# Another order of work, and another PSUM layout, for the first sequence of an attention and feed-forward kernel

## The chip, the cores and the metric

The kernel runs on one core of a Trainium2 chip. The metric is the device time of one execution in microseconds (us), the median of several runs. A profile of one execution gives every instruction's engine, start and length; its times count from the first instruction. PE is the matmul engine (TensorE), PEld its loading of weights, DVE is VectorE, ACT ScalarE, POOL GpSimd, SP the engine that issues most transfers.

## The reference

All data is float32. Attention with a threshold over 8 sequences of 576 tokens with 8 heads of 64, and then two matrices with an ELU between them. The weights come as 64-bit floats and are converted on the chip.

```python
# q, k, v: (8, 8, 576, 64);  tau = 0.02;  w_in: (512, 2048);  w_out: (2048, 512)
scores = (q @ k.transpose(0, 1, 3, 2)) / sqrt(64)
thresh = scores.max(-1, keepdims=True) - tau
scores = where(scores >= thresh, scores, -1e9)
attn = exp(scores - scores.max(-1, keepdims=True))
attn = attn / (attn.sum(-1, keepdims=True) + 1e-9)
x = (attn @ v).transpose(0, 2, 1, 3).reshape(4608, 512)
h = x @ w_in
out = where(h > 0, h, exp(minimum(h, 0)) - 1) @ w_out
```

## The kernel before

The kernel has three stages. In the first, the first sequence's attention is computed alone, since there is nothing yet to put through the two matrices; some weights are converted meanwhile. In the second, attention goes on beside the first sequence's matrices and the rest of the conversions. In the third and longest, attention and matrices share the engines until only matrices are left. The change touches the first stage.

A sequence has four pairs of heads, and a pair five steps: i = 0 to 3 are 128 queries of two heads each, and i = 4 holds the last 64 queries of both heads as one block of 128 rows, handled as one head. So a sequence has 20 steps. For each step and head the first stage does the following (S = 576, HALF = 288, P = 128; cuts are marked):

```python
psum = {"t": tile_pool(name="ps_t", bufs=2, space=PSUM)}      # transposes and values: 2 banks
psum["s"] = tile_pool(name="ps_s0", bufs=3, space=PSUM)       # scores: 3 tiles of 2 banks
# ...
def scores(pr, i, hs):
    # ...
    if "f" in psum and not apart:                              # second stage: one tile for both heads
        both = psum["s"].tile([P, 2, 2, 512], FP32, name="sc")
        scs = {h: both[:, h] for h in hs}
    else:                                                      # first and third stage: one tile a head
        scs = {h: psum["s"].tile([P, 2, 512], FP32, name="sc") for h in hs}
    for a in range(2):
        for h in hs:
            # ... r: the 64 partitions of head h
            nc.tensor.matmul(scs[h][:, a, :HALF], qs[r], kT[r, k0 : k0 + HALF], start=True, stop=True)

def exponentials(pr, i, hs):
    nc.vector.tensor_reduce(st["mx"][:, cs], src[:, :, :, :HALF], axis=AX.XY, op=ALU.max)
    nc.gpsimd.tensor_scalar(st["nb"][:, cs], st["mx"][:, cs], nkeep, 1.0, ALU.mult, ALU.mult)
    nc.gpsimd.tensor_scalar(st["th"][:, cs], st["mx"][:, cs], 1.0, ntau, ALU.mult, ALU.add)
    for h in hs:
        e = att.tile([P, 2, HALF], FP32, name="e")
        nc.scalar.activation(e, st[h][:, :, :HALF], AF.Exp, bias=st["nb"][:, h : h + 1], scale=keep)

def masks(pr, i, hs):
    for h in hs:                                               # keeps e where the score is over the threshold; sums
        nc.vector.scalar_tensor_tensor(wv, sc[:, :, :HALF], st["th"][:, h : h + 1], e, ALU.is_ge, ALU.mult,
                                       accum_out=sm[:, h : h + 1])
    nc.vector.tensor_scalar(sm[:, cs], sm[:, cs], 1e-9, None, ALU.add)
    nc.vector.reciprocal(rs[:, cs], sm[:, cs])

def normalize(pr, i, hs):
    for h in hs:
        nc.gpsimd.tensor_scalar(wv, wv, st["rs"][:, h : h + 1], 1.0, ALU.mult, ALU.mult)
```

The weighted scores w are then transposed on TensorE in three portions of four, four and one block (turn_parts), each into a tile of psum["t"] that ScalarE copies out. After steps 1 and 4 of a pair the values are multiplied in (17 matmuls into a tile of psum["t"]); part 0 covers steps 0 and 1, part 1 the steps 2 to 4.

```python
def values(pr, part):
    pv = psum["t"].tile([P, 512], FP32, name="pv", tag="rt")
    nc.tensor.matmul(pv[:, :n], vd, wT[:, :, NC], start=True, stop=False, skip_group_check=True)
    for c in range(NC):
        for h in range(2):
            nc.tensor.matmul(pv[h * D : (h + 1) * D, g0 * T : g1 * T], vm[:, h, c], ..., start=False, ...)
    return lambda: values_out(pr, part, pv)                    # copies pv out on ScalarE
```

The loop of the first stage goes head by head, and the compiler's scheduler may move instructions in it:

```python
load(0); prep(0); load(1)
begin(*heads[0])                                 # begin: scores and exponentials; finish: masks and normalize
for n, (pr, i, hs) in enumerate(heads):          # 36 heads: one entry for each head of each step
    if n + 1 < len(heads):
        begin(*heads[n + 1])
    # ... loads of weights
    if n >= 12 and n % 4 == 0:
        convert_w()                              # six pieces of 128 x 512 weights in this stage
    finish(pr, i, hs)
    if len(turned) > 1:
        behind(*turned.popleft())                # values
    if n and hs == [0]:
        turn(*heads[n - 1][:2])                  # transposes of the step before
        turned.append(heads[n - 1][:2])
    if hs == [1]:
        ahead(pr, i + 1)                         # loads, and q and k of the next pair
```

Of the kernel before, what the change touches and what calls it, by code (L numbers as in the profile page):

```python
# [10 lines left out]
FP32 = mybir.dt.float32  # L11
# [8 lines left out]
def kernel(  # L20
# [47 lines left out]
    first = ExitStack()  # L68
    psum["s"] = first.enter_context(tc.tile_pool(name="ps_s0", bufs=3, space=PSUM))

# [7 lines left out]
    tau_sb = const.tile([P, 1], FP32, name="tau_sb")  # L78
    nc.sync.dma_start(tau_sb, tau.to_broadcast([P, 1]))
    pos = const.tile([P, 1], FP32, name="pos")  # L80
    nc.vector.tensor_scalar(pos, tau_sb, 0.0, None, ALU.is_ge)
    keep = const.tile([P, 1], FP32, name="keep")
    nc.vector.tensor_scalar(keep, pos, SCALE, None, ALU.mult)
    nkeep = const.tile([P, 1], FP32, name="nkeep")
    nc.vector.tensor_scalar(nkeep, pos, -SCALE, None, ALU.mult)
    far = const.tile([P, 1], FP32, name="far")
    nc.vector.tensor_scalar(far, pos, -FAR, FAR, ALU.mult, ALU.add)
    ntau = const.tile([P, 1], FP32, name="ntau")
    nc.vector.tensor_tensor(ntau, tau_sb, far, ALU.max)
    nc.vector.tensor_scalar(ntau, ntau, -1.0 / SCALE, None, ALU.mult)  # L90

# [64 lines left out]

    def convert_w():
        i = progress[1]
        if i >= progress[0]:
            return  # L160
        for f in (convert_top, convert_rest, convert_add, convert_abs, convert_end):
            f(i)
        load_w()


    raws, pairs = {}, {}


    def load(pr, parts=("qm", "km", "v"), shared=False):
        b, j = divmod(pr, NPAIR)  # L170
        tiles = raws.setdefault(pr, {})
        for name, src in (("qm", q), ("km", k)):
            if name not in parts:
                continue
            m = tiles[name] = raw.tile([P, S // T, T], FP32, name="qm" if shared else name)
            for i in range(2):
                for d in range(2):
                    r = (2 * i + d) * T
                    nc.sync.dma_start(
                        m[r : r + T],  # L180
                        src[b, 2 * j + i].rearrange("(j t) d -> t j d", t=T)[:, :, d * T : (d + 1) * T],
                    )
        if "v" not in parts:
            return
        vm = tiles["vm"] = raw.tile([P, 2, NC, D], FP32, name="vm", bufs=2)
        vd = tiles["vd"] = vds[pr % NVD]
        for i in range(2):
            vh = v[b, 2 * j + i]
            nc.sync.dma_start(vm[:, i], vh[:MAIN].rearrange("(c p) d -> p c d", p=P))
            r = slice(i * TAIL, (i + 1) * TAIL)  # L190
            nc.sync.dma_start(vd[r, r], vh[MAIN:])
# [25 lines left out]

    wTs, xts, open_steps, turns = {}, {}, {}, {}
    apart = []


    def scores(pr, i, hs):
        qT, kT, qd = pairs[pr]
        if hs[0] == 0:
            open_steps[pr, i] = {
                **{x: small.tile([P, 2], FP32, name=x) for x in ("mx", "nb", "th", "sm", "rs")},
            }
        st = open_steps[pr, i]
        if "f" in psum and not apart:
            both = psum["s"].tile([P, 2, 2, 512], FP32, name="sc")  # L230
            scs = {h: both[:, h] for h in hs}
        else:
            scs = {h: psum["s"].tile([P, 2, 512], FP32, name="sc") for h in hs}
        for a in range(2):
            for h in hs:
                k0 = a * HALF + (0 if h else TAIL)
                r, qs = (slice(h * D, (h + 1) * D), qT[:, i * P : (i + 1) * P]) if i < NC else (slice(0, P), qd)
                nc.tensor.matmul(scs[h][:, a, :HALF], qs[r], kT[r, k0 : k0 + HALF], start=True, stop=True)  # L238
        if len(hs) == 2 and not apart:
            st["both"] = both  # L240
        for h in hs:
            st[h] = scs[h]

    def exponentials(pr, i, hs):
        st = open_steps[pr, i]
        cs = slice(hs[0], hs[-1] + 1)
        src = st["both"] if len(hs) == 2 else st[hs[0]].unsqueeze(1)
        nc.vector.tensor_reduce(st["mx"][:, cs], src[:, :, :, :HALF], axis=AX.XY, op=ALU.max)
        nc.gpsimd.tensor_scalar(st["nb"][:, cs], st["mx"][:, cs], nkeep, 1.0, ALU.mult, ALU.mult)  # L249
        nc.gpsimd.tensor_scalar(st["th"][:, cs], st["mx"][:, cs], 1.0, ntau, ALU.mult, ALU.add)  # L250
        for h in hs:
            e = att.tile([P, 2, HALF], FP32, name="e")
            nc.scalar.activation(e, st[h][:, :, :HALF], AF.Exp, bias=st["nb"][:, h : h + 1], scale=keep)  # L253
            st[h] = st[h], e

    def masks(pr, i, hs):
# [5 lines left out]
        for h in hs:  # L262
            sc, e = st.pop(h)
            wv = w[:, h * S : (h + 1) * S].rearrange("p (a n) -> p a n", a=2)
            nc.vector.scalar_tensor_tensor(wv, sc[:, :, :HALF], st["th"][:, h : h + 1], e, ALU.is_ge, ALU.mult,  # L265
                                           accum_out=sm[:, h : h + 1])
# [3 lines left out]
    def normalize(pr, i, hs):  # L270
        st = open_steps[pr, i]
        for h in hs:
            wv = st["w"][:, h * S : (h + 1) * S]
            nc.gpsimd.tensor_scalar(wv, wv, st["rs"][:, h : h + 1], 1.0, ALU.mult, ALU.mult)  # L274

    def transpose(dst, src):
# [11 lines left out]
    def turn_parts(pr, i):  # L288
        w = open_steps.pop((pr, i))["w"]
        wT, g0 = turned_tile(pr, i)  # L290
# [4 lines left out]
        def room():  # L295
            return psum["t"].tile([P, NC, P], FP32, name="rt", tag="rt")

# [240 lines left out]

    def begin(*step):
        scores(*step)  # L540
        exponentials(*step)

    def finish(*step):
        masks(*step)
        normalize(*step)

    def ahead(pr, i):
        if i == 2 and pr + 1 < NP:
            prep(pr + 1)
        if i == 3 and pr + 2 < NP:  # L550
            load(pr + 2, ("qm", "km"))
        if i == 3 and pr + 1 < NP and pr:
            load(pr + 1, ("v",))

    load(0)
    prep(0)
    load(1)

    heads = [(pr, i, [h]) for pr, i in steps[:per_seq] for h in heads_of(i)]
    turned = deque()  # L560
    begin(*heads[0])
    for n, (pr, i, hs) in enumerate(heads):
        if n + 1 < len(heads):
            begin(*heads[n + 1])
        if n == 2:
            load_w()
            load_w()
        if n >= 12 and n % 4 == 0:
            convert_w()
        finish(pr, i, hs)  # L570
        if len(turned) > 1:
            behind(*turned.popleft())
        if n and hs == [0]:
            turn(*heads[n - 1][:2])
            turned.append(heads[n - 1][:2])
        if hs == [1]:
            ahead(pr, i + 1)
    first.close()
    for name, bufs in (("s", 1), ("f", 2)):
        psum[name] = banks.enter_context(tc.tile_pool(name=f"ps_{name}", bufs=bufs, space=PSUM))  # L580

    while len(turned) > 1:
        behind(*turned.popleft())

# [161 lines left out]
    with tc.manual_schedule():  # L746
# [335 lines left out]

        def max_of(pr, i, h):
            st = open_steps[pr, i]
            nc.vector.tensor_reduce(st["mx"][:, h : h + 1], st[h][:, :, :HALF], axis=AX.XY, op=ALU.max)  # L1085

        def bound_of(pr, i, h):
            st = open_steps[pr, i]
            nc.gpsimd.tensor_scalar(st["th"][:, h : h + 1], st["mx"][:, h : h + 1], 1.0, ntau, ALU.mult, ALU.add)  # L1089

        def exp_of(pr, i, h):
            st = open_steps[pr, i]
            nc.scalar.mul(st["nb"][:, h : h + 1], st["mx"][:, h : h + 1], nkeep)  # L1093
            e = att.tile([P, 2, HALF], FP32, name="e")
            nc.scalar.activation(e, st[h][:, :, :HALF], AF.Exp, bias=st["nb"][:, h : h + 1], scale=keep)  # L1095
            st[h] = st[h], e

        def mask_of(pr, i, h):
            st = open_steps[pr, i]
            if h == 0:  # L1100
                st["w"] = wpool[0].tile([P, 2 * S], FP32, name="w")
            sc, e = st.pop(h)
            wv = st["w"][:, h * S : (h + 1) * S].rearrange("p (a n) -> p a n", a=2)
            nc.vector.scalar_tensor_tensor(wv, sc[:, :, :HALF], st["th"][:, h : h + 1], e, ALU.is_ge, ALU.mult,  # L1104
                                           accum_out=st["sm"][:, h : h + 1])

        def reciprocal_of(pr, i, hs):
            st = open_steps[pr, i]
            cs = slice(hs[0], hs[-1] + 1)
            nc.vector.tensor_scalar(st["sm"][:, cs], st["sm"][:, cs], 1e-9, None, ALU.add)  # L1110
            nc.vector.reciprocal(st["rs"][:, cs], st["sm"][:, cs])  # L1111

        begun = [0.0]
# [100 lines left out]
        spaces = [raw.tile([P, S // T, T], FP32, name="qm")]  # L1214
        spaces += [att.tile([P, 2, HALF], FP32, name="e") for _ in range(2)]
        spaces = [x.rearrange("p a n -> p (a n)") for x in spaces]
        spaces += [raw.tile([P, 2, NC, D], FP32, name="vm", bufs=2).rearrange("p h c d -> p (h c d)") for _ in range(2)]
        w = wpool[0].tile([P, 2 * S], FP32, name="w")
# [54 lines left out]
```

## Time and profile before

| | |
|---|---|
| time, median of 3 runs | 1387.97 us (1381.94 to 1388.02) |
| profiled execution, span | 1379.2 us |
| busy: PE, DVE, POOL, ACT | 1333.0, 1060.4, 834.1, 624.7 us |
| mean granted clock of TensorE | 0.996 |
| first score matmul | 8.44 us |
| last mask of the first sequence | from 102.09 us, 0.82 us long |
| first max of the second sequence | 106.33 us |

Busy times are sums over the whole span; PE's is modelled, and its matmuls overlap. The first stage is some 8% of the span. A record of a float32 score or value matmul counts twice (x4 is two matmuls); a transpose counts once. In a group or a piece of the timeline, "L265" is the line of the kernel, then come engine, operation, the tiles written and read, and shapes; in brackets stands how long the engine was idle before, and what ended that.

### The profile page before, as it was taken

The numbers are of one execution on the slowest core, as the hardware profiler recorded it, in microseconds if no ns is written. First come the engines' busy times: TensorE is split into PE (matmuls) and PEld (weight loads), VectorE is DVE, ScalarE is ACT, GpSimd is POOL, SyncE is SP. The second block draws the span as 40 slices with busy tenths as digits, with TensorE's granted clock in tenths as the row PEclk, the third lists the DMA queues.
The fourth block names the chain that finished last, engine by engine and source line by source line (L and its number), as shares of the span: only waits on it lengthen the run. The fifth ranks groups of instructions, "written<-read, shape, count | busy, mean of one in ns | idle before, by whom it ended". The sixth has DMA issues, their size and how long they took to land.

```text
span 1379.2 us, 21964 instructions
## 1 busy us (share of the span) xinstructions
PE 1333.0 (97%) x6566; PEld 989.4 (72%) x6566; DVE 1060.4 (77%) x2364; ACT 624.7 (45%) x1371; POOL 834.1 (60%) x1345
## 2 busy tenths in 40 slices
PE   7897989999999999999999999999999999999998
PEld 4554745747777777777777777777777777888886
DVE  6787885988878887888788878888888875545433
ACT  4675655225454544445453635364535452312320
POOL 4667774878657564757475747665575656525423
PEclk9999999999999999999999999999999999999999
DMA  5245452688788989798889888897889885321211
GB/s 114 58 92 148 133 148 44 189 244 253 228 257 229 261 226 257 209 257 247 236 229 256 245 224 245 221 263 215 232 229 270 215 255 166 122 69 62 95 58 31
DMA packets 316342, 259.82 MB, mean 188 GB/s; under 512 B 208320, under 2 KB 272320, under 8 KB 316224
## 3 DMA queue, kind: packets, MB, share of 16 engines
q1 hardware_dynamic: 316224, 258.42, 67.4%
q8 instruction: 53, 0.87, 0.3%
q14 instruction: 65, 0.53, 0.1%
HBM read 167.84 MB, written 90.51 MB: 187 GB/s over the span
## 4 chain that ended last, share of the span: by engine, by line
PE 74%; DVE 9%; ACT 5%; POOL 4%; DMA 3%; issue 3%; SPq 1%; DVEq 0%; POOLq 0%; ACTq 0%
PE f L1001 27%; PE f L846 20%; PE sc L238 11%; PE pv L388 8%; PE pv L384 2%; PE f L435 2%; PE f L475 2%; ACT e L1095 2%; DVE w L265 2%; DMA there<-x 2%; ACT e L253 1%; DVE mx L1085 1%; PE rt L277 1%; POOL wtop L143 1%; POOL w L274 1%
## 5 line engine op out<-in xcount | busy, mean ns | idle before, releaser
L274 POOL TENSOR_SCALAR w<-w,rs 128x576 f32<-128x576 f32 x288 | 246.1, 860 | 108.1 <-DVE rs L1111 75.2
L1085 DVE TENSOR_REDUCE mx<-sc 128x1 f32<-128x576 f32 x207 | 148.0, 751 | 83.4 <-PE sc L238 83.4
L238 PE MATMUL sc<-kT,qT 64*128 64x288 f32 x1024 | 182.3, 441 | 20.8 <-DVE w L265 11.5
L348 DVE STREAM_TRANSPOSE x<-w 128x512 f32<-128x512 f32 (+1 forms) x350 | 182.5, 567 | 8.2 <-POOL w L274 8.2
L1093 ACT ACTIVATE nb<-mx,nkeep 128x1 f32<-128x1 f32 x207 | 61.4, 297 | 253.2 <-DVE mx L1085 253.2
L1095 ACT ACTIVATE e<-sc,nb,keep 128x576 f32<-128x576 f32 x207 | 172.0, 831 | 6.9
L1104 DVE SCALAR_TENSOR_TENSOR w<-sc,th,e 128x576 f32<-128x576 f32 x207 | 163.1, 810 | 8.7 <-ACT e L1095 0.4
L238 PEld LDWEIGHTS sc<-kT,qT 64*128 64x128 f32 x1024 | 100.8, 191 | 85.4 <-issue 52.4
L846 PE MATMUL f<-xt,sw 128*128 128x256 f32 x512 | 128.9, 389 | 0.5 <-DVE g L868 0.5
L846 PE MATMUL f<-xt,w_in_sb 128*128 128x256 f32 x512 | 124.5, 382 | 0.3 <-ACT w L860 0.2
L1089 POOL TENSOR_SCALAR th<-mx,ntau 128x1 f32<-128x1 f32 x207 | 54.4, 264 | 112.1 <-DVE mx L1085 111.8
L846 PE MATMUL f<-x,w_in_sb 128*128 128x256 f32 x448 | 109.0, 382 | 5.5 <-ACT g L912 5.5
L846 PEld LDWEIGHTS f<-xt,sw 128*128 128x128 f32 x512 | 93.3, 190 | 28.9 <-issue 13.5
L253 ACT ACTIVATE e<-sc,nb,keep 128x576 f32<-128x576 f32 x81 | 65.1, 830 | 103.5 <-POOL nb L249 102.6
L846 PEld LDWEIGHTS f<-xt,w_in_sb 128*128 128x128 f32 x512 | 96.1, 190 | 18.9 <-ACT xs L400 4.6
L1001 PE MATMUL f<-w_out_sb,s 128*128 128x256 f32 x448 | 109.4, 387 | 0.0
L1001 PE MATMUL f<-w_out_sb,g 128*128 128x256 f32 x448 | 107.2, 382 | 0.0
L1001 PE MATMUL f<-t,s 128*128 128x256 f32 x448 | 106.6, 380 | 0.3 <-POOL s L938 0.3
L846 PEld LDWEIGHTS f<-x,w_in_sb 128*128 128x128 f32 x448 | 84.1, 190 | 21.2 <-ACT g L912 10.2
L1001 PEld LDWEIGHTS f<-w_out_sb,s 128*128 128x128 f32 x448 | 82.3, 190 | 23.0 <-issue 13.2
L1001 PEld LDWEIGHTS f<-w_out_sb,g 128*128 128x128 f32 x448 | 84.0, 190 | 15.9 <-ACT ge L879 3.1
L865 POOL TENSOR_TENSOR u<-u,w 128x256 f32<-128x256 f32 x64 | 48.9, 765 | 76.4 <-ACT u L860 76.4
(162 smaller groups left out, 2572.2 us busy)
## 6 DMA issues: line engine op xcount, KB each, us to landing
there<-x SPq DMA_DIRECT2D x500, 144.0 KB, 4.3
wTb<-there SPq DMA_DIRECT2D x75, 576.0 KB, 4.7
wTa<-there SPq DMA_DIRECT2D x50, 576.0 KB, 4.4
sw<-win_sums SPq DMA_DIRECT2D x62, 384.0 KB, 4.6
t<-wout_sums SPq DMA_DIRECT2D x45, 512.0 KB, 5.5
qm<-in_q_dram SPq DMA_DIRECT2D x128, 72.0 KB, 4.2
vm<-in_v_dram SPq DMA_DIRECT2D x64, 128.0 KB, 4.3
wst<-in_moe_w_in_dram SPq DMA_DIRECT2D x16, 512.0 KB, 4.5
```

The costliest lines, as they stand in the source:

```text
L238: nc.tensor.matmul(scs[h][:, a, :HALF], qs[r], kT[r, k0 : k0 + HALF], start=True, stop=True)
L253: nc.scalar.activation(e, st[h][:, :, :HALF], AF.Exp, bias=st["nb"][:, h : h + 1], scale=keep)
L274: nc.gpsimd.tensor_scalar(wv, wv, st["rs"][:, h : h + 1], 1.0, ALU.mult, ALU.mult)
L348: nc.vector.transpose(x[:, :, c0 : c0 + nc_], src.rearrange("p (c g n) -> p g c n", c=nc_, n=T))
L388: nc.tensor.matmul(pv[h * D : (h + 1) * D, g0 * T : g1 * T], vm[:, h, c], wT[:, g0:g1, h * (NC + 1) + c], start=False, stop=(c == NC - 1), ...
L846: nc.tensor.matmul(loc["banks"][place], left[:, j], right[:, j], start=(begins and j == 0), stop=(j == 1), skip_group_check=True)
L1001: nc.tensor.matmul(place(m), lhs, rhs, start=(begins and v == 0), stop=(v == RU - 1), skip_group_check=True)
L1085: nc.vector.tensor_reduce(st["mx"][:, h : h + 1], st[h][:, :, :HALF], axis=AX.XY, op=ALU.max)
L1089: nc.gpsimd.tensor_scalar(st["th"][:, h : h + 1], st["mx"][:, h : h + 1], 1.0, ntau, ALU.mult, ALU.add)
L1093: nc.scalar.mul(st["nb"][:, h : h + 1], st["mx"][:, h : h + 1], nkeep)
L1095: nc.scalar.activation(e, st[h][:, :, :HALF], AF.Exp, bias=st["nb"][:, h : h + 1], scale=keep)
L1104: nc.vector.scalar_tensor_tensor(wv, sc[:, :, :HALF], st["th"][:, h : h + 1], e, ALU.is_ge, ALU.mult, accum_out=st["sm"][:, h : h + 1])
```

## The change

The first stage gets an order that is fixed by hand, as the other two have. The scores of a step are now written in three parts of 192 keys, with a pitch of 256, so that two whole steps of one head fit into three banks, and those of both heads into six. The scores run two steps ahead and the maxes and exponentials one step ahead of the masks; both heads' matmuls are issued in turns. Reciprocals are taken for both heads at once. TensorE gets idle transposes of the identity (28 at the start, 8 in steps 0, 2 and 4 of a pair), whose results nobody reads, so that it is not idle for long. At the start, k comes over ScalarE's queue, beside q on SP's. The number of weight pieces converted in this stage stays six.

```diff
-    psum["s"] = first.enter_context(tc.tile_pool(name="ps_s0", bufs=3, space=PSUM))
+    psum["s"] = first.enter_context(tc.tile_pool(name="ps_s0", bufs=1, space=PSUM))
+    fours = [psum["s"].tile([P, 2, 3, 256], FP32, name=f"sc{x}") for x in range(2)]
 ...
+        n, pitch = (S // 3, 256) if "f" not in psum else (HALF, 512)
 ...
+        elif "f" not in psum:
+            scs = {h: fours[h][:, (pr + i) % 2, :, :n] for h in hs}
 ...
-        for a in range(2):
+        for a in range(S // n):
             for h in hs:
 ...
-                nc.tensor.matmul(scs[h][:, a, :HALF], qs[r], kT[r, k0 : k0 + HALF], start=True, stop=True)
+                nc.tensor.matmul(scs[h][:, a], qs[r], kT[r, k0 : k0 + n], start=True, stop=True)
 ...
         def room():
-            return psum["t"].tile([P, NC, P], FP32, name="rt", tag="rt")
+            rt = psum["t"].tile([P, NC, P], FP32, name="rt", tag="rt")
+            for _ in range(spare.pop() if spare else 0):
+                transpose(rt[:, 0], ident)
+            return rt
 ...
+    with tc.manual_schedule():
+        load(0, ("qm",))
+        nc.sync.dma_start(tau_sb, tau.to_broadcast([P, 1]))
+        load(0, ("km",), queue=nc.scalar)
+        load(0, ("v",))
+        load(1)
+        rt = psum["t"].tile([P, NC, P], FP32, name="rt", tag="rt")
+        for _ in range(28):
+            transpose(rt[:, 0], ident)
 ...
+        def exps(n):
+            for h in heads_of(steps[n][1]):
+                max_of(*steps[n], h)
+                exp_of(*steps[n], h, True)
+                bound_of(*steps[n], h)
+
+        for n in range(2):
+            scores(*steps[n], [0, 1])
+        exps(0)
 ...
+        for n in range(per_seq):
+            pr, i = steps[n]
+            hs = heads_of(i)
+            x = progress[1]
+            for h in hs:
+                mask_of(pr, i, h)
+            reciprocal_of(pr, i, hs)
+            out_values = None
+            if n:
+                copies()
+                if i not in (1, 3):
+                    spare.append(8)
+                for part in turned[1:]:
+                    part()()
+            if n > 1 and i in (1, 3):
+                out_values = values(steps[n - 2][0], 0 if i == 3 else 1)
+            if n + 2 < per_seq:
+                scores(*steps[n + 2], heads_of(steps[n + 2][1]))
 ...   (conversions of weights on ScalarE)
+            normalize(pr, i, [0])
+            if n + 1 < per_seq:
+                exps(n + 1)
+            if out_values:
+                out_values()
+            if len(hs) == 2:
+                normalize(pr, i, [1])
+            if n + 1 < per_seq:
+                turned = turn_parts(pr, i)
+                copies = turned[0]()
 ...   (q and k of the next pair at i = 1 and 2, conversions on VectorE and GpSimd, loads)
```

max_of, exp_of, bound_of, mask_of and reciprocal_of are the parts of exponentials and masks above for a single head; max_of reads that head's scores of one step, in one instruction.

## The prediction

> **What bounds the kernel now.** I read the page first. Over the whole span TensorE has a busy share of 97% and carries the chain that ended last, but that is an average over three stages. The change touches only the first sequence (20 steps of attention), so I asked for the busy time in stretches that follow its four pairs of heads; after each start, length and sum the columns are busy us and instructions by engine.
>
> ```profile
> 8.40:28.00 19.60, 17.89 (x57) 12.49 (x58) 13.16 (x35) 8.80 (x14) 8.36 (x24) 1.00 0.53 116
> 28.00:52.00 24.00, 22.36 (x122) 13.14 (x120) 19.89 (x55) 16.85 (x35) 17.10 (x34) 1.00 0.24 50
> 52.00:76.00 24.00, 21.31 (x114) 12.11 (x113) 18.28 (x53) 15.66 (x33) 13.94 (x31) 1.00 0.34 81
> 76.00:100.00 24.00, 22.48 (x118) 13.30 (x116) 20.40 (x57) 18.04 (x38) 17.05 (x34) 1.00 0.41 101
> ```
>
> A pair (four steps of two heads, one of one head) takes about 23.7 us: the score matmuls of the last step start at 26.4, 50.4, 74.4 and 97.0. VectorE is busy 18 to 20 of 24 us and TensorE 21 to 22; each waits for the other in turn. The groups of instructions between 20 and 100 us give unit costs and waits.
>
> ```profile
> L265 DVE SCALAR_TENSOR_TENSOR w<-sc,th,e 128x576 f32<-128x576 f32 x31 | 25.0, 807 | 7.5 <-PE rt L277 4.1 <-POOL w L274 1.2 <-ACT e L253 0.9
> ...
> L248 DVE TENSOR_REDUCE mx<-sc 128x1 f32<-128x576 f32 x31 | 23.1, 749 | 7.8 <-PE sc L238 7.7
> ```
>
> Max 0.75 us, mask 0.81 us a head; VectorE loses only 7.7 us in 80 waiting for scores, because the score buffers are three separate tiles: a head's scores are computed while another head's are read. The last mask of the sequence:
>
> ```profile
> 102.09 0.82 DVE L265 SCALAR_TENSOR_TENSOR w<-sc,th,e 128x576 f32<-128x576 f32 x1 [0.53 <-POOL th L250]
> ...
> 106.33 1.36 DVE L248 TENSOR_REDUCE mx<-sc 128x2 f32<-128x1152 f32 x1 [2.48 <-PE sc L238]
> ```
>
> So the first sequence ends at 102.9 us, and the second's first max starts at 106.3. All of the change lies before that point; what follows is the same code, and I let it only shift.
>
> The second sequence shows the rule on which I stake most. There both heads' scores lie in one tile, in separate banks.
>
> ```profile
> 125.67 1.55 ACT L253 ACTIVATE e<-sc,nb,keep 128x576 f32<-128x576 f32 x2 [2.06 <-POOL nb L249]
> ...
> 127.34 0.82 DVE L265 SCALAR_TENSOR_TENSOR w<-sc,th,e 128x576 f32<-128x576 f32 x1 [1.10 <-ACT e L253]
> ...
> 128.96 1.24 PE L238 MATMUL sc<-kT,qT 64*128 64x288 f32 x8 [0.24 <-DVE w L265]
> ...
> 130.13 0.70 PE L384 MATMUL pv<-wTa,vd 128*128 128x256 f32 x2
> ...
> 130.76 1.95 PE L388 MATMUL pv<-wTa,vm 128*64 128x256 f32 x16
> ...
> 132.64 0.66 PE L277 MATMUL rt<-ident,w 128*128 128x128 f32 x4
> ```
>
> The first head's mask needs the first exponential (done about 126.5) but starts at 127.34, 0.12 after the second one ended (127.22). It is so in every such step (118.47 and 118.59, 136.34 and 136.46). In the third stage, with a tile per head, a mask starts before the other head's exponential ends (616.94 against 617.52). So accesses by different engines to one PSUM tile run in program order, even where they touch different banks.
>
> **What the Trainium skill says.** "PSUM — Partial Sum Buffer", PSUM bank collisions raise a hardware error: no two engines may be in the same bank and quadrant at once, whatever columns they touch, so the program has to order them. The new layout puts the third part of one step and the first part of the next into one bank; they must be ordered. The trace agrees in kind, with a coarser order, as above. "TensorE: Matmul & The Clock Gate", Part 3: matmuls on different row groups run side by side. Here four matmuls of two heads in turns take 1.24 us (8 records), and two of one head 1.23 or 1.24 (4 records): agreed. The same page, Part 1: the array's clock is halved after idle time. At 19.35 one score matmul takes 1.33 us, at 34.49 0.75, though the granted clock reads 1.00 in both stretches: consistent with it, and the reason for the idle transposes.
>
> **The change part by part.** Start: k comes over a second queue, and 28 idle transposes warm TensorE. The transfers share the same engines (busy 0.57 of the first 8.4 us), so I let scores start at 7.8 instead of 8.44. Two steps' scores take 1.23 + 1.0 us warm; max at 10.1; the first exponential at 11.3; second mask ends at 13.9 (before: 14.9).
>
> Loop: in program order step n does: masks(n), scores(n+2), max(n+1), exponentials(n+1). Scores(n+2) and max(n+1) of a head are now in one tile, so max(n+1) must wait for all of scores(n+2), which must wait for masks(n). "Two steps ahead" is therefore undone: the scores come back onto VectorE's path. From the end of the second mask, with durations of this trace: scores start +0.07 (120.14 to 120.21), last 1.23 (the two heads side by side), +0.04 to the max at 1.34, max to 2.09, +0.15 to nb, +0.30 to the exponential at 2.54, 0.83 long, +0.12 to the mask at 3.49; the second mask starts 0.74 later and ends at **5.05 us**. A step with one head: 4.31. The reciprocals (0.33) and the normalizing lie beside this.
>
> Values: at i=1 and i=3 the value matmuls stand ahead of scores(n+2) on TensorE. They need the buffer of the previous step's second transposes, so they start near +0.5. They last 2.5 us (130.13 to 132.64) in part 0, 3.14 in part 1 (91.50 to 94.64). Scores then start at +3.0 or +3.65 and not +0.07: **+2.95 and +3.6 us** on the path. In the step after, 8 idle transposes and the next turning wait for the values' buffer, which ScalarE empties only behind the exponentials; scores come later by about 0.8 (after part 0) and 1.1 us (after part 1). Weight conversion: VectorE has a gap of 0.7 us behind the maxes; 1.8 us at i=4 adds 1.1 a pair (0.4 in pair 0). The q and k transposes (0.78) fit.
>
> Sum. Pair 0: 3 x 5.05 + (4.31 + 2.95) + (5.05 + 0.8 + 0.4) = 28.7. Pairs 1 and 2, each: 5.05 + (5.05 + 3.6) + (5.05 + 1.1) + 7.26 + (5.05 + 0.8 + 1.1) = 34.1. Pair 3 to its last mask: 5.05 + 8.65 + 6.15 + 7.26 = 27.1. From 13.9: 13.9 + 28.7 + 68.2 + 27.1 = 137.9, against 102.9: +35 us. The handover to the second sequence has fewer transposes and no values in front of its scores: -1.5. That is +33.5, or 1421. What is saved (reciprocals for two heads at once, about 1 us a pair of VectorE; scores of both heads side by side, about 5 us a pair of TensorE) is off this path.
>
> **The rivals.** (1) Each half of the tile is ordered by itself. Then scores are hidden, a step is about 4.1 us, a pair 21, limited by VectorE's own 20.9 (9 x 1.56 + 1.7 + 1.55 + 3.6 of conversions), and the time falls by 8 to 10 to 1378. For it: this is plainly the intent, and the long tuning of such a kernel rarely keeps a loss. Against it: the shared bank and the 127.34. (2) Order by bank only: in odd steps the shared part is the first one written, so half the steps save 0.7 us: 1412. (3) The loop is as I say, but values slip into idle time: 16 x 5.05 + 4 x 4.31 is already as long as the old sequence, and the time is 1390 to 1398. Against it: TensorE works in order, and values come first. (4) TensorE's clock falls in the gaps despite the idle transposes: some us more.
>
> **Range and chances.** My sum gives 1421; the rivals below it are likelier than the one above, so I take **1417 us**, with 1391 to 1432. 2% slower is 1415.7, right below it. Rival 1 or 3 has near 30% together; of the rest somewhat over two thirds lies above 2%. Faster by 2% would need 28 us out of 102.9, below what VectorE alone needs: faster 0.02, same 0.46, slower 0.52.
>
> **What would show it.** Right: max waits for the scores of TensorE some 40 us in the first sequence (7.7 before), max starting about 0.04 after a score matmul that belongs to the later step; a two-head step of 5 us without and 8 us with values; the second sequence's first max near 140 us, and equal lengths after it. Wrong: maxes that start while scores run, steps near 4.1 us and a first max near 97.

## The result, and the profile after

| | before | after |
|---|---|---|
| time, median of 4 runs | 1385.13 us (1381.94 to 1388.02) | 1437.31 us (1434.42 to 1441.99) |
| ratio to before, 95% interval | | 1.0377 (1.0341 to 1.0412) |
| profiled execution, span | 1379.2 us | 1432.1 us |
| mean granted clock of TensorE | 0.996 | 0.975 |
| last mask of the first sequence ends | 102.9 us | 152.6 us |
| second sequence's first max | 106.33 us | 158.67 us |
| from there to the end | 1272.9 us | 1273.4 us |

The change costs 3.8%, and nearly all of it lies ahead of the second sequence's first max: 52.3 of the 52.9 us between the two spans. From there on the two kernels are equally long to within 0.6 us.

What is new stands in the page's row of granted clock, in 40 slices of the span. Before, all forty digits were 9.

```profile
PEclk8887899999999999999999999999999999999999
```

A slice is 35.8 us: the first four lie in the first sequence, and the fifth holds its end. Four stretches of the sequence (start, length, busy time and instructions of PE, PEld, DVE, ACT and POOL, granted clock, DMA share, GB/s); they are not whole pairs:

```profile
8.30:36.50 28.20, 21.23 (x120) 15.35 (x121) 15.21 (x40) 9.91 (x17) 10.62 (x29) 0.76 0.49 109
36.50:69.40 32.90, 21.26 (x126) 14.97 (x126) 18.15 (x42) 15.07 (x32) 13.38 (x30) 0.84 0.09 15
69.40:105.00 35.60, 25.29 (x151) 16.23 (x151) 16.90 (x38) 13.81 (x30) 14.67 (x27) 0.81 0.21 52
105.00:140.00 35.00, 26.08 (x133) 16.45 (x133) 15.53 (x37) 13.55 (x27) 13.28 (x24) 0.71 0.19 48
```

From reciprocal to reciprocal, pairs 1 and 2 take 38.9 and 41.5 us instead of about 24. VectorE works about half of the time instead of four fifths of it, and TensorE's clock is 0.71 to 0.84 of full speed where it had been 1.00. The groups of instructions between 20 and 130 us (count, busy us, mean ns, then the idle time ahead of them and what ended it):

```profile
L273 DVE TENSOR_REDUCE mx<-sc 128x1 f32<-128x576 f32 x27 | 19.3, 753 | 49.6 <-PE sc L235 49.6
...
L419 PE MATMUL pv<-wTa,vm 128*64 128x256 f32 x48 | 10.3, 603 | 0.0
...
L419 PE MATMUL pv<-wTb,vm 128*64 128x320 f32 x32 | 8.1, 679 | 0.0
```

The same value matmuls before, between 20 and 100 us:

```profile
L388 PE MATMUL pv<-wTb,vm 128*64 128x320 f32 x48 | 7.1, 439 | 0.0
L388 PE MATMUL pv<-wTa,vm 128*64 128x256 f32 x48 | 5.8, 385 | 0.0
```

A max is as long as before (753 ns, 749 before), but VectorE now waits 49.6 us in 110 for scores ahead of the maxes, where it was 7.7 in 80. And a record of the value matmuls takes 603 and 679 ns on average, where it was 385 and 439; the unit costs of the prediction were taken from such matmuls. One step with values, from the timeline:

```profile
83.93 1.98 PE L235 MATMUL sc<-kT,qT 64*128 64x192 f32 x12 [2.26 <-DVE w L295]
...
90.60 1.65 PE L415 MATMUL pv<-wTb,vd 128*128 128x384 f32 x2 [0.46 <-ACT wTa L321]
...
92.17 4.54 PE L419 MATMUL pv<-wTb,vm 128*64 128x320 f32 x16
...
96.64 1.25 PE L235 MATMUL sc<-kT,qT 64*128 64x192 f32 x12
...
97.92 1.42 DVE L273 TENSOR_REDUCE mx<-sc 128x1 f32<-128x576 f32 x2 [7.93 <-PE sc L235]
```

The last mask of step 11 (steps count from 0) ended at 89.58. The values stand ahead of the scores two steps ahead and take 6.04 us (90.60 to 96.64); then come the scores of step 13, and 0.03 us behind them the maxes of step 12, whose own scores had been there for 12 us (83.93 to 85.91). VectorE has waited 7.93 us. The granted clock of that same stretch (in pieces of 1 us; the clock is the number behind the five busy times):

```profile
85.00:86.00 1.00, 0.91 (x10) 0.61 (x6) 0.38 (x2) 0.00 (x0) 0.75 (x1) 1.00 0.00 0
86.00:87.00 1.00, 0.79 (x4) 0.42 (x4) 1.00 (x3) 0.21 (x1) 0.51 (x2) 0.70 0.00 0
87.00:88.00 1.00, 0.00 (x0) 0.00 (x0) 0.94 (x3) 0.80 (x2) 0.85 (x3) 0.50 0.00 0
...
95.00:96.00 1.00, 1.00 (x8) 0.37 (x4) 0.00 (x0) 0.00 (x0) 0.00 (x0) 0.50 0.00 0
96.00:97.00 1.00, 1.00 (x8) 0.36 (x6) 0.00 (x0) 0.00 (x0) 0.00 (x0) 0.68 0.00 0
97.00:98.00 1.00, 1.00 (x14) 0.78 (x11) 0.08 (x1) 0.00 (x0) 0.00 (x0) 1.00 0.00 0
```

The clock is halved from about 86.4 to about 96.6 us (the rows with 0.70 and 0.68 hold the change), so all of these values ran at half speed.

Two causes are therefore to be told apart: the wait of the maxes for later scores with whatever stands ahead of those (my theory), and TensorE's clock (my rival 4). For either I also had to show that it is this cause and not something that comes with it.

### The profile page after: what moved, and what is told of

It reads as the page before. It is cut to its first block, busy times and chain, and to the rows that moved or that the text cites. A ratio compares the mean times of both kernels' runs of the same rounds, so it can differ in the third digit from the quotient of the medians.

```text
span 1432.1 us, 22304 instructions
## 1 busy us (share of the span) xinstructions
PE 1353.3 (94%) x6754; PEld 1010.3 (71%) x6754; DVE 1064.6 (74%) x2332; ACT 624.5 (44%) x1371; POOL 837.7 (58%) x1345
## 4 chain that ended last, share of the span: by engine, by line
PE 76%; DVE 9%; ACT 5%; issue 3%; DMA 3%; POOL 3%; SPq 1%; DVEq 0%; POOLq 0%; ACTq 0%
PE f L1069 27%; PE f L914 20%; PE sc L235 11%; PE pv L419 9%; PE pv L415 3%; PE f L506 2%; DVE mx L273 2%; PE f L466 2%; ACT e L286 2%; PE rt L305 2%; ACT e L248 1%; DVE w L260 1%; DMA there<-x 1%; DMA qm<-in_q_dram 1%; DVE wtop L135 1%
## 5 line engine op out<-in xcount | busy, mean ns | idle before, releaser
L273 DVE TENSOR_REDUCE mx<-sc 128x1 f32<-128x576 f32 x243 | 173.8, 752 | 143.9 <-PE sc L235 143.9
L286 ACT ACTIVATE e<-sc,nb,keep 128x576 f32<-128x576 f32 x243 | 200.9, 831 | 80.7 <-POOL nb L282 73.8
L295 DVE SCALAR_TENSOR_TENSOR w<-sc,th,e 128x576 f32<-128x576 f32 x243 | 191.7, 812 | 13.5 <-POOL w L269 2.0
L235 PE MATMUL sc<-kT,qT 64*128 64x288 f32 (+1 forms) x1088 | 165.6, 420 | 22.1 <-DVE w L260 10.4
L235 PEld LDWEIGHTS sc<-kT,qT 64*128 64x128 f32 x1088 | 97.0, 190 | 84.1 <-issue 52.7
L277 POOL TENSOR_SCALAR th<-mx,ntau 128x1 f32<-128x1 f32 x243 | 67.4, 278 | 111.4 <-DVE mx L273 110.9
L1069 PEld LDWEIGHTS f<-t,s 128*128 128x128 f32 x448 | 84.1, 190 | 13.7 <-POOL s L1006 2.7
```

The source lines that it names most:

```text
L235: nc.tensor.matmul(scs[h][:, a], qs[r], kT[r, k0 : k0 + n], start=True, stop=True)
L273: nc.vector.tensor_reduce(st["mx"][:, h : h + 1], st[h], axis=AX.XY, op=ALU.max)
L286: nc.scalar.activation(e, st[h], AF.Exp, bias=st["nb"][:, h : h + 1], scale=keep)
L295: nc.vector.scalar_tensor_tensor(wv, sc, st["th"][:, h : h + 1], e, ALU.is_ge, ALU.mult, accum_out=st["sm"][:, h : h + 1])
L1069: nc.tensor.matmul(place(m), lhs, rhs, start=(begins and v == 0), stop=(v == RU - 1), skip_group_check=True)
```

## The experiments

All times are medians, and a ratio is always that to the kernel before, run on the same chip (1383.99 to 1385.74 us there). The line numbers shift by a few lines from kernel to kernel.

**Is it the tile that two steps share?** The scores have six banks, which the program lays out with 512 columns each. A tile of its own for each of two steps and two heads leaves one bank for a step's 576 scores, which do not fit. So in both of the next two runs the three parts of 192 keys lap over each other by 32 columns: every instruction keeps its size, 64 of a row's 576 scores are lost. The two runs differ only in the tiles.

```diff
-fours = [psum["s"].tile([P, 2, 3, 256], FP32, name=f"sc{x}") for x in range(2)]
+fours = [psum["s"].tile([P, 2, 512], FP32, name=f"sc{x}") for x in range(2)]                 # shared
+fours = [[psum["s"].tile([P, 512], FP32, name=f"sc{x}{y}") for y in range(2)] for x in range(2)]  # apart
 ...   (the three parts are written and read at columns 0, 160 and 320)
```

Shared, expected:

> The changed kernel with the three parts of 192 keys written at columns 0, 160 and 320 of one bank of 512 columns, so that the last 32 columns of a part are overwritten by the next: 64 of the 576 scores of a row are lost, the output is not the reference's, but every instruction keeps its size. One tile for each head still holds two steps, each step now in a bank of its own. Theory (the order is kept for the whole tile, whatever the banks): as the changed kernel, 1430 to 1442 us, and VectorE waits about 50 us for scores in the window 20:130. Rival (the order is kept for banks, and it was the bank shared by two steps that bound): as the next run, below 1400.

Measured: 1436.53 us, ratio 1.0374 (1.0326 to 1.0421), the changed kernel's own. In this run two steps of a head share a tile but no bank, so the shared bank isn't the cause.

Apart, expected:

> As the run before it (three parts of 192 keys lapped in one bank, 64 of 576 scores of a row lost, all instructions of the same size), but each head and each step has a tile of its own, four tiles in four banks. Theory (the wait of the maxima for the scores two steps ahead comes from the tile that the two steps share): that wait is gone, 1375 to 1400 us, and VectorE waits under 12 us for scores in the window 20:130. Rival (TensorE is too slow in its low clock, or the chain over exponentials binds anyway): above 1420 us.

Measured: 1390.08 us, ratio 1.0033 (1.0021 to 1.0045). The waits of VectorE's maxes for scores between 20 and 130 us (sum in us, times, longest), first shared and then apart:

```profile
DVE mx L279 <- PE sc L241: 50.5, 15, 7.9
```

```profile
DVE mx L279 <- PE sc L241: 7.8, 4, 3.2
```

And from the timeline of the run with tiles apart, one end of a step:

```profile
21.70 0.17 DVE L308 RECIPROCAL rs<-sm 128x2 f32<-128x2 f32 x1
21.79 1.40 DVE L279 TENSOR_REDUCE mx<-sc 128x1 f32<-128x576 f32 x2
...
21.91 1.14 PE L241 MATMUL sc<-kT,qd 128*128 128x192 f32 x6
```

The maxes run beside the scores two steps ahead, as the change intended; here a step without values takes 4.0 us. Nothing but the tiles differs, so some 46 of the 52 us are shown to hang on the shared tile. Not all of that is the wait itself: with the tiles apart the granted clock is higher as well, 0.82 to 0.95 in four stretches from 8 to 140 us, where it is 0.71 to 0.88 with the tile shared.

**Values ahead of scores.** One thing turned round in the changed kernel, with its whole layout:

```diff
-            if n > 1 and i in (1, 3):
-                out_values = values(steps[n - 2][0], 0 if i == 3 else 1)
             if n + 2 < per_seq:
                 scores(*steps[n + 2], heads_of(steps[n + 2][1]))
+            if n > 1 and i in (1, 3):
+                out_values = values(steps[n - 2][0], 0 if i == 3 else 1)
```

> Of the changed kernel one thing is turned round: in the steps that also multiply values, the scores two steps ahead are issued to TensorE before the values instead of behind them. Theory (the maxima of the next step wait for the scores two steps ahead, since both lie in one PSUM tile, and so for whatever TensorE has to do ahead of those scores): the eight groups of values of 4 to 6 us each leave that path, though a part of each comes back as later transposes. 1405 to 1418 us instead of 1437, and VectorE waits for scores about 25 us in the window 20:130 instead of 49.6. Rival (the slow clock or the number of instructions is what costs, and the order does not matter): within 5 us of 1437, and about 50 us of waiting.

Measured: 1412.26 us, ratio 1.0181 (1.0157 to 1.0205); the maxes wait 34.2 us for scores. The time is as expected, 25 to 27 us gained; the wait fell less than I had said.

The opposite turn puts the scores behind the exponentials and leaves the values where they are:

```diff
-            if n + 2 < per_seq:
-                scores(*steps[n + 2], heads_of(steps[n + 2][1]))
 ...
             if n + 1 < per_seq:
                 exps(n + 1)
+            if n + 2 < per_seq:
+                scores(*steps[n + 2], heads_of(steps[n + 2][1]))
```

> The changed kernel with the scores two steps ahead issued behind the exponentials of the next step instead of ahead of them; values stay where they are, now ahead of both. Theory (accesses of one tile run in the order of the program): the maxima no longer wait for scores, so values run beside the exponentials; but scores now wait for the exponentials and the masks of the next step for the scores, 1.3 us in every step. A step of two heads 5.5 to 6.0 us without values and about the same with them; 1400 to 1412 us in all. Rival (only the values' place counts): as the run with the values behind the scores, 1412, with steps of 5.0 us. Rival (the order of issue does not set the order of the accesses): 1437.

Measured: 1421.00 us, ratio 1.0266 (1.0247 to 1.0285), outside the expected range. The mechanism is there: no wait of a max for scores is left among the longest, and in its place the masks wait between 20 and 130 us:

```profile
DVE w L295 <- PE sc L235: 46.3, 17, 6.1
```

My estimate made the steps too short: most two-head steps without values took 6.5 to 8.0 us (at i = 3, 5.5 to 5.8), and those behind values of part 1 7.7 to 10.1; in one of these the values took 5.6 us. The granted clock was 0.76 to 0.90 here, which my estimate had left out. How much of the excess is the clock isn't shown, since this order wasn't run with the clock held up.

**The clock.** First the changed kernel without its idle transposes:

```diff
-        for _ in range(28):
-            transpose(rt[:, 0], ident)
 ...
-                if i not in (1, 3):
-                    spare.append(8)
```

> The changed kernel without its idle transposes: the 28 at the start and the 8 in three of five steps are left out, nothing else. Theory (they keep TensorE's clock from falling further but do not hold it up, and where they stand they mostly run while TensorE would wait): the granted clock of the first 140 us falls from 0.71-0.84 to about 0.6, and the time rises by 0 to 12 us over 1437. Rival (they stand in front of the scores and so delay them by 0.8 to 1.1 us in twelve steps): 1425 to 1430, with the clock about as it was.

Measured: 1433.96 us, ratio 1.0354 (1.0316 to 1.0392), which overlaps with that of the changed kernel; the clock in four stretches from 8 to 140 us is 0.75 to 0.78. Neither side was right. The idle transposes as the change has them neither hold the clock up nor cost much.

Then idle transposes that can do it. In the run with shared lapped tiles (1436.53) two banks are free. There the idle transposes get a tile of their own, so that they need not wait for ScalarE to empty a buffer, and they are more (the two come together):

```diff
+        calm = psum["s"].tile([P, P], FP32, name="calm")
+        def idle(n):
+            for _ in range(n):
+                transpose(calm, ident)
 ...
-                if i not in (1, 3):
-                    spare.append(8)
+                idle(18)
                 for part in turned[1:]:
                     part()()
 ...
+            if n and i == 0:
+                idle(18)
             if n + 2 < per_seq:
                 scores(*steps[n + 2], heads_of(steps[n + 2][1]))
```

> The run with three parts lapped in one bank and one tile for both steps of a head (1436.5 us), with one thing changed: the idle transposes get a bank of their own, so that they wait for no buffer, and there are 18 in every step ahead of the second part of the turning, and 18 more ahead of the scores two steps ahead in the first step of each pair. They are to fill TensorE's gaps of 2 to 2.8 us, behind which the trace shows the granted clock at 0.50. Theory (the term that was mis-sized is the length of values and scores, taken at full clock, where they ran at half): the granted clock of the first 140 us rises to 0.93 or more, values take 2.5 and 3.1 us again, and the time falls by 12 to 18 us to 1418 to 1425. Rival (something else made the loop longer than predicted): within 5 us of 1436.5, or more because of the added work.

Measured: 1413.49 us, ratio 1.0212 (1.0196 to 1.0228): 23 us less than the run it is built on, more than expected. Its stretches, and a step with values of part 1:

```profile
36.00:70.00 34.00, 30.94 (x255) 25.10 (x253) 19.37 (x45) 16.94 (x36) 15.61 (x34) 1.00 0.23 50
70.00:105.00 35.00, 31.55 (x259) 25.14 (x257) 20.74 (x49) 18.07 (x38) 18.58 (x35) 1.00 0.28 67
```

```profile
82.82 0.91 PE L421 MATMUL pv<-wTb,vd 128*128 128x384 f32 x2 [0.57 <-ACT wTa L327]
83.67 2.37 PE L425 MATMUL pv<-wTb,vm 128*64 128x320 f32 x16
85.97 1.25 PE L241 MATMUL sc<-kT,qT 64*128 64x192 f32 x12
```

The clock is back at 1.00, and the values take 3.15 us (82.82 to 85.97), which is the prediction's 3.14. TensorE has more to do here, 368 idle transposes between 20 and 130 us, and the kernel is faster for it. Whether it is their number or their own tile that makes them work here isn't separated.

Both turns together, the free idle transposes and the values behind the scores:

> The run with a bank of its own for idle transposes (1413.5 us, one lapped tile for both steps of a head), with the values issued behind the scores two steps ahead as well. Theory (two causes that add: values ahead of scores, 2.5 and 3.1 us at full clock less about half that comes back behind them, seven times; and the clock): 1397 to 1406 us. What is left over the kernel before, 12 to 20 us, is then the wait for the scores themselves in each step. Rival (with the clock up, the values' place no longer matters): within 4 us of 1413.5.

Measured: 1404.09 us, ratio 1.0138 (1.0125 to 1.0151), as expected. In the changed kernel the values' place was worth 25 us, with the clock held up 9; short values take less away. The 19 us that remain over the kernel before fit the theory: with the values and the clock out of the way, the maxes still wait 31.8 us for scores between 20 and 130 us (7.7 before, between 20 and 100). With the tiles apart and the values in this place, the next run takes 1388.14 us.

**Can the order be mended?** With lapped tiles apart, two more runs looked for what still holds the loop. One has the values behind the scores as above:

> Four lapped tiles in four banks as in the run of 1390 us (64 of 576 scores of a row lost), with the values issued behind the scores two steps ahead as well. Theory (what that run still lost were values ahead of scores, which show one step later in 7 to 9 us long steps): 1375 to 1384 us. Rival (those long steps come from the conversions and the turning): within 4 us of 1390.

Measured: 1388.14 us, ratio 1.0022 (1.0012 to 1.0032): the rival's side. Its interval overlaps with that of the first run with tiles apart (1.0021 to 1.0045), so the gap of 2 us may be none. The other also leaves out the idle transposes of the loop and issues the exponentials to ScalarE ahead of the remaining copies:

```diff
-                for part in turned[1:]:
-                    part()()
+                rest = [part() for part in turned[1:]]      # transposes only
 ...   (no idle transposes in the loop, and no values here)
                 exps(n + 1)
+            for f in rest:
+                f()                                         # their copies
+            if n > 1 and i in (1, 3):
+                out_values = values(steps[n - 2][0], 0 if i == 3 else 1)
```

> Four lapped tiles in four banks (64 of 576 scores of a row lost), with the eight idle transposes of a step left out, and with the exponentials of the next step issued to ScalarE ahead of the copies of the remaining turning and ahead of the values' copies; values behind both. Theory (what the runs of 1390 and 1388 us still lost beside a free-running loop is that exponentials stood behind copies that waited for TensorE): 1370 to 1383 us. Rival (a pair of 25 us is what TensorE, ScalarE and VectorE need together): 1386 to 1392.

Measured: 1394.40 us, ratio 1.0069 (1.0050 to 1.0089), slower instead of faster. By its waits between 20 and 130 us another queue holds it:

```profile
ACT xt L432 <- PE pv L425: 23.4, 7, 4.9
```

ScalarE stands at the copy of the values until they are done, and the next exponentials queue behind that copy. So even a loop free of the shared tile isn't shorter than the old one in these orders: steps of 4.0 us without values, but 6 to 9 us around them.

With the change's own layout, all scores kept, I tried to give the tile the order in which the data comes: behind the masks of step n the scores of n + 2, then their maxes and exponentials.

```diff
             for h in hs:
                 mask_of(pr, i, h)
+            if n + 2 < per_seq:
+                scores(*steps[n + 2], ...)                  # one head's parts, then the other's
 ...
-                exps(n + 1)
+                exps(n + 2, ...)                            # four buffers for exponentials
 ...   (then the remaining turning, its copies, the values; no idle transposes)
```

> The changed kernel's score tiles as they are, with another order: in each step, behind the masks, scores two steps ahead (one head's three parts and then the other's), then their maxima and exponentials two steps ahead as well, and the remaining turning and the values behind the scores; no idle transposes in the loop; the exponentials get two more buffers. Theory (one tile's accesses run in the order of the program, so the order should be the one in which the data comes): what is left is one chain for each head, mask 0.8, scores 0.75, maximum 0.75, bias 0.3, exponential 0.83, about 3.6 us with its handovers, and the two heads take turns in it; VectorE's own 20.4 us a pair bind. 1368 to 1385 us, below or level with the kernel before. Rival (the layout itself costs, by slow clock or by TensorE's work): 1395 or more.

Measured: 1432.32 us, ratio 1.0344 (1.0324 to 1.0365). My expectation was far off. Its timeline, from all engines:

```profile
73.33 1.22 PE L416 MATMUL pv<-wTa,vd 128*128 128x256 f32 x2 [1.39 <-ACT wTb L322]
...
74.48 3.68 PE L420 MATMUL pv<-wTa,vm 128*64 128x256 f32 x16
...
78.96 1.67 PE L236 MATMUL sc<-kT,qT 64*128 64x192 f32 x12
...
80.24 0.76 DVE L274 TENSOR_REDUCE mx<-sc 128x1 f32<-128x576 f32 x1 [6.97 <-PE sc L236]
```

A mask had ended at 73.3, but TensorE had just begun values that had themselves waited for ScalarE's copies, and the clock was 0.50. So the next run moved the values directly behind the scores:

> The run with scores, maxima and exponentials two steps ahead (1432 us) with one thing changed: the values stand directly behind the scores two steps ahead on TensorE, ahead of the remaining turning, instead of behind the turning and its copies. Theory (in that run the masks ended about 5 us before the next scores could start, because TensorE was still at values that had themselves waited for ScalarE's copies): values begin 2 to 3 us earlier, steps with values shrink from 8-11 to 6-7.5 us, 1398 to 1415 us in all. Rival (the place of values does not matter, the chain of each head does): within 6 us of 1432.

Measured: 1427.74 us, ratio 1.0309 (1.0290 to 1.0329), hardly better, and on the rival's side. The maxes wait less for scores, 27.3 us between 20 and 130 us instead of 49.1, but now the masks wait, 24.4 us in all:

```profile
67.32 0.82 DVE L296 SCALAR_TENSOR_TENSOR w<-sc,th,e 128x576 f32<-128x576 f32 x1 [5.90 <-PE rt L306]
```

There are two buffers for the weighted scores w, and a mask needs the one that the turning of two steps ago, now behind the values, has yet to read. With the clock at 0.67 to 0.76 values are long here too. I read this from the waits; a third buffer for w or a warm clock in this order wasn't tried.

**The start alone**, in the kernel before:

```diff
-    load(0)
-    prep(0)
-    load(1)
+    load(0, ("qm",))
+    nc.sync.dma_start(tau_sb, tau.to_broadcast([P, 1]))
+    load(0, ("km",), queue=nc.scalar)
+    load(0, ("v",))
+    rt = psum["t"].tile([P, NC, P], FP32, name="rt", tag="rt")
+    for _ in range(28):
+        transpose(rt[:, 0], ident)
+    prep_q(0)
+    prep_k(0)
+    read_tau()      # tau's small instructions on VectorE
+    copy_k(0)
+    copy_q(0)
+    load(1)
```

> The kernel before with the start of the changed one alone: the first keys' transfers on ScalarE's queue beside those of the queries, tau's small instructions behind the two turnings, and 28 idle transposes while the first data comes. Theory (the prediction's -0.5 to -1 us at the start): first score at 8.3 us, the end 0 to 3 us earlier, 1382 to 1385.5 beside 1385.4. Rival (the start gains nothing, since the loop behind it waits for something else): within 0.5 us.

Measured: 1382.15 us beside 1383.99, ratio 0.9986 (0.9977 to 0.9995), as expected, and just clear of no gain. TensorE's timeline at the start:

```profile
1.46 5.62 PE L274 MATMUL rt<-ident 128*128 128x128 f32 x28 [1.46 <-POOL ident masks.py:199]
7.97 2.20 PE L235 MATMUL sc<-kT,qT 64*128 64x288 f32 x12 [0.89 <-DVE pos L82]
```

The first scores start at 7.97 instead of 8.44, and their first twelve records take 2.20 us instead of 4.20. The second sequence's first max comes at 104.40, 1.9 us earlier than before. This is the one part of the change that is worth keeping, and the only kernel with all its scores that beats both.

## Why the prediction was right and wrong

The direction, to which I gave a chance of only 0.52, and the mechanism were right, the size was not: 1437.31 us lies above the range that ends at 1432. Step lengths in us, from the starts of the reciprocals, for the pairs 1 and 2 (the columns of two numbers are pair 1 and pair 2):

| step that ends | predicted | after | shared lapped tiles, clock held up |
|---|---|---|---|
| i = 1, no values ahead | 5.05 | 5.0, 5.0 | 6.0, 5.4 |
| i = 2, behind values of part 1 | 8.65 | 11.0, 12.0 | 8.6, 8.6 |
| i = 3 | 6.15 | 7.3, 6.0 | 5.3, 5.3 |
| i = 4, behind values of part 0 | 7.26 | 8.8, 10.1 | 7.2, 7.3 |
| next i = 0 | 6.95 | 6.8, 8.5 | 6.3, 6.3 |
| pair | 34.1 | 38.9, 41.5 | 33.4, 32.9 |

- **"Accesses by different engines to one PSUM tile run in program order"**: right. Shared against apart gives 46 us, with the same sizes and no bank shared between steps, and with the scores issued behind the maxes the waits changed over to the masks.
- **A step of two heads 5.05 us**: right, 5.0 where no values stand ahead.
- **Values stand ahead of the scores and on the path**: right in kind; moved behind, they give 25 us back.
- **"They last 2.5 us (130.13 to 132.64) in part 0, 3.14 in part 1 (91.50 to 94.64)"**: this is the step that failed. The durations come from a kernel whose clock was 1.00 there, and I put them into a loop that makes TensorE wait. In the changed kernel they took 4.1 to 4.8 us in part 0 and 5.1 to 6.04 in part 1; the six groups that stand ahead of this sequence's scores are together 13 us longer than I had them. With the clock held up, 3.15 us came back, a pair took 33.4 and 32.9 us instead of 38.9 and 41.5, and the time fell by 23 us. I had this as the fourth rival and gave it "some us more".
- **The idle transposes**: I took their purpose for their effect. Leaving them out changed nothing outside the intervals, though the first scores gained from them (last section).
- **Pair 3, 27.1 us, and the handover of -1.5**: two smaller errors that partly cancel. The last two steps have no scores two steps ahead, so nothing held the very last step: 3.8 us (148.8 to 152.6) instead of 7.26. But those values did not vanish. They ran from 149.77 to 154.53, past the last mask and ahead of the second sequence's scores, and the way from the last mask to the next first max became 6.1 us; before it was 3.4, and I had said 1.9.
- **The start**: scores at 8.32 and not 7.8, the second mask at 14.4 and not 13.9; half of the expected gain.

The sum of the prediction (33.5 us more, with the second first max near 140: 1421 on the 1387.97 us known then, 1418.6 on the 1385.13 measured beside the change) thus comes closer to the kernel with the clock held up: that one had its max at 137.18 and took 1413.5 us. It is no exact match: its steps i = 1, which have 18 more idle transposes ahead of the scores, and i = 3 differ from my terms by up to 0.9 us in either direction. The rivals below my theory (halves ordered by themselves, order by bank, values in idle time) are all excluded. I had shaded the number from 1421 to 1417 for their sake, and left 11 us above it for the only rival that came.

Not settled: why the loop with tiles apart, 1388 to 1394 us, doesn't beat the old one. ScalarE's wait for values is seen there, but no run took it away.

## What to carry to other kernels

Software that runs ahead needs a tile for each step in flight: here two steps in one tile saved banks but gave back the whole lead, since a max of the nearer step waited for scores of the further one. When a change puts waits on TensorE, don't take its unit costs from the trace of before: price its work at half clock as well, and let the range hold both. Idle instructions meant to keep an engine's clock up may do nothing where they wait for the work's own buffers: 72 such transposes had no effect on the time, 368 in a tile of their own gave 23 us, and which of the two differences did it is open.

## What the runs showed that I had not expected

- The granted clock fell to 0.50 at about 86.4 us and stayed there to 96.6, although TensorE was never idle for more than 2.8 us between 74 and 102 us. When it fell, TensorE had worked for 2.5 us, almost unbroken, since a gap of 2.26 us (81.67 to 83.93); when it rose, TensorE had hardly paused since 88.8. The Trainium skill, "TensorE: Matmul & The Clock Gate", Part 1, has the cold state follow at least one idle window of some 3.4 us; here there was no such gap. What decides the moment isn't shown.
- Transposes of the identity do hold the clock up: with 18 in a step, 2.13 us, it read 1.00 from 36 to 105 us and 0.99 to 140, where the run it is built on, with its 8 in three of five steps, had 0.84, 0.76 and 0.71. The same page, Part 4, says of transposes that they don't count as work in the same way; these runs differ. So do the first scores of the changed kernel: behind the 28 transposes their 24 records take 2.60 us (from 8.32), and in the run without idle transposes 4.59 us (from 8.23). The granted clock reads 1.00 from 8 to 12 us in both, so there only the durations tell slow from fast.
- Idle transposes alone made a kernel 23 us faster: 368 of them between 20 and 130 us instead of 72.
